# An attention and two feed-forward layers in one kernel: ScalarE's casts ordered behind its last copy, and one more block's rounding on VectorE

## The chip, the cores and the metric

The kernel runs on one core of a Trainium2 chip. The core has TensorE (PE in the profile; its weight loads are PEld), VectorE (DVE), ScalarE (ACT), GpSimd (POOL) and SyncE (SP), which issues all transfers of this kernel. Each engine works through its own queue strictly in order; an instruction that waits holds up all that stand behind it on its engine. The metric is the device time of one execution in microseconds (us), lower is better; the median of several runs is compared.

## The reference

Three parts follow each other, all in float32, on 4 x 576 = 2304 tokens of width 512.

```python
B, H, S, D = 4, 8, 576, 64
scores = (1.0 / np.sqrt(D)) * np.matmul(q, k.transpose(0, 1, 3, 2))
cum = np.cumsum(np.maximum(s, 0.0), axis=-1)
bias = -(cum[:, :, :, None] - cum[:, :, None, :])
scores = np.where(causal, -1e9, scores + np.minimum(bias, 0.0))
attn = softmax(scores)                       # max subtracted, sum + 1e-9
x = np.matmul(attn, v)                       # -> (2304, 512)
h = x @ w_in                                 # 512 -> 2048
x = (h - np.tanh(h)) @ w_out                 # 2048 -> 512
h = (x @ w1) * (x @ w2) @ w3                 # 512 -> 1024 -> 1024
out = h @ w_out2                             # 1024 -> 512
```

## The kernel before

**Stages.** The first phase (to about 385 us) does attention and, woven into it, the first half of the first feed-forward layer: 8 of the 16 slices of w_in and w_out. The second phase does the other 8 slices (tiles named hb, yb) and prepares weights; the third does the second feed-forward layer. The change touches the first phase alone.

**Attention.** Work goes by pairs of heads, numbered 0 to 31 (`p.n`); pairs 0 to 7 are of the first batch and are computed without a split (`p.first`). For a pair, TensorE makes score tiles `s` in PSUM; VectorE takes the maxima (`nm`); ScalarE takes the exponentials (`pr`) and their sums; TensorE transposes them (`pt`); ScalarE copies the transposes to SBUF (`pf`, line 310; from the second batch on VectorE copies those of unit B2); TensorE multiplies them with v (`pv`); VectorE multiplies `pv` by the inverted sums `rb`, which come back through DRAM (`rt`, `rd`, `rb`), and so writes x into `xy` (line 364). From pair 8 on GpSimd adds most of the bias (`pr`, line 206, two to four operations a pair) and sets the causal mask (line 218). All tiles `s`, `pt`, `pv` and `pri` share five PSUM banks.

**Feed-forward.** x is taken in nine blocks of 256 tokens (blk 0 to 8), each as four column chunks. For full precision every operand is split in two float32r parts, a rounded high part and the rest, and every product is three matmuls (high by high, high by low, low by high). `cut_x` splits a chunk of x into `xhl`: ScalarE casts the high part (line 64), VectorE subtracts for the low part (line 65). For each of 8 slices f of a block TensorE makes `h` (12 matmuls over the four chunks in order), ScalarE takes tanh (`th`, line 460), VectorE subtracts (line 463), g is split into `gh` and `gl`, and TensorE adds g times w_out to `y`. `split` casts on ScalarE and subtracts on GpSimd, unless told otherwise; blocks 0 and 1 split g that way, blocks 2 to 8 do both on VectorE:

```python
if blk < 2:
    split(gh, gl, t)
else:
    split(gh, gl, t, hi=nc.vector.tensor_copy, lo=nc.vector.tensor_sub)
```

**Weights.** `convert` turns raw 64-bit weights into float32 on VectorE in three operations (lines 88, 91 and 93, tile `cvt`), casts the high part on ScalarE and subtracts on GpSimd. `park` does the same for weights that are written to DRAM until the second phase (`park_win`, `park_wout`).

**Order.** TensorE's order is written out by hand (a table of steps, `at`). The other engines' order is set by a scheduler that goes by its own estimate of times; `in_turn(i, behind)` adds an order between two instructions that it must keep (no semaphore is waited for, it only restrains where the scheduler may place i). So casts and copies stand on ScalarE where the scheduler expects them to be ready.

Of the kernel before, what the change touches and what calls it, by code (L numbers as in the profile page):

```python
# [15 lines left out]
P = 128  # L16
# [8 lines left out]
BLK = 256  # L25
# [12 lines left out]
def tile_kernel(ctx: ExitStack, tc: tile.TileContext, qk, v, s, w_in, w_out, w1, w2, w3t, w_o2, outT):  # L38
    nc = tc.nc
# [10 lines left out]
    xy = cp.tile([P, NC, NT], F32, tag="xy", name="xy")  # L50
# [45 lines left out]

    def convert(raw, name, w=None, lo=None, behind=None):
        t = plain(raw, name, behind)
        w = slot(name) if w is None else w
        split(w[:, 0, :], w[:, 1, :], t, lo=lo)  # L100
        return w
# [21 lines left out]
    with ExitStack() as actx:  # L123
# [20 lines left out]

        latest, least, last_exp, paces = [None], [None], [None], []
        PACED = 70
# [159 lines left out]
        def evacuate(p, j, e):  # L306
            pieces, pt, at = p.pf[j, e]

            pf = a2.tile([P, {"B1": 512, "B2": 416}.get(j, 384)], F32, tag=f"pf{0 if j == 'A' else j[1]}".replace("3", "0"), name=f"pf{p.n}_{j}_{e}")
            (nc.vector.tensor_copy if j == "B2" and not p.first else nc.scalar.copy)(pf[:, :at], pt[:, :at])  # L310
            p.pf[j, e] = pieces, pf, at
# [28 lines left out]
        def store(p):  # L340
            m = 2 * p.ni
            p.rt = a2.tile([6, P], F32, tag="rt", name=f"rt{p.n}")
            nc.scalar.copy(p.rt[:m], p.pt[:m, :P])
            p.rd = dr.tile([2, 3 * P], F32, tag="rd", name=f"rd{p.n}", bufs=4)
            nc.sync.dma_start(p.rd[:, :p.ni * P].rearrange("t (i c) -> t i c", c=P), p.rt[:m])
# [23 lines left out]
        def conversions(fs):  # L369
# [5 lines left out]
            for m, (d, f, src, n) in enumerate(todo):  # L375
                d[f] = convert(raws.pop(0), n, behind=least[0])
                if m + 2 < len(todo):
                    raws.append(load_raw(*todo[m + 2][2:], behind=latest[0]))
                yield
# [20 lines left out]
        def ffn():  # L400
# [6 lines left out]
            def cut_x(blk, lo):  # L407
                xs = cut.setdefault(blk, [])
                c, c0 = len(xs), blk * BLK
                x = f2.tile([P, 2, BLK], F32R, tag="xhl", name=f"xhl{blk}_{c}", bufs=6)  # L410
                split(x[:, 0, :], x[:, 1, :], xy[:, c, c0:c0 + BLK], lo=lo)
                xs.append(x)

            for blk in range(NB):
# [30 lines left out]
                for f in range(F1):  # L445
# [16 lines left out]
                    def rest(t=t, hh=hh, gh=gh, gl=gl, blk=blk):  # L462
                        nc.vector.tensor_sub(t, hh, t)  # L463
                        if blk < 2:
                            split(gh, gl, t)
# [561 lines left out]
```

## Time and profile before

| | us |
|---|---|
| median of 3 runs | 954.67 |
| lowest and highest | 949.22, 955.17 |
| the profiled execution | 953.33 |
| its span, first to last instruction | 951.5 |

The profile is of one execution: 1.8 us of its own time lie outside its span. The rows further below are of that execution, and times in them count from the start of the span. PE was busy in 97% of the span at a mean granted clock of 0.989; DVE in 68%, ACT in 48%, POOL in 24%. A row of the timeline has its start, its duration, engine, line, operation, what it writes and reads with shapes, and in square brackets how long the engine sat idle before it and what released it. Buffer numbers are left out of names there.

### The profile page before, as it was taken

Reading aid. Unit: us, or ns where it says so; the run is one execution under the profiler, and the core shown is the slowest. Engines: PE = TensorE matmul, PEld = TensorE weight load, DVE = VectorE, ACT = ScalarE, POOL = GpSimd, SP = SyncE. Lnnn points to the kernel's source line nnn. Section 1 sums busy time; section 2 is a strip of 40 time slices with the busy share of each in tenths; the row PEclk is TensorE's granted clock in tenths of the full one; section 3 lists DMA queues with packets and bytes.
Section 4 is the critical chain, followed back from the end, with each engine's and each line's share of the span. In section 5 each row is a group of like instructions: output and inputs, shape, how many; then the busy total and the mean of one; then the engine's idle time right before and its main releaser. Section 6 shows DMA issues by size and latency. Waiting matters only on the chain.

```text
span 951.5 us, 16425 instructions
## 1 busy us (share of the span) xinstructions
PE 921.0 (97%) x6022; PEld 803.0 (84%) x6025; DVE 646.5 (68%) x1394; ACT 452.2 (48%) x1061; POOL 231.0 (24%) x219
## 2 busy tenths in 40 slices
PE   8889999899999999999999999998999999999998
PEld 4467778788888889998888888986899999999997
DVE  7677767687787866767999887673145546744654
ACT  4457877777777743324544343332124232433233
POOL 2245756556565410000000000020024111311100
PEclk9799999999999999999999999999999999999999
DMA  5555365435444523499788644668399767776746
GB/s 161 192 160 171 112 199 189 170 126 183 147 167 145 179 91 98 147 355 362 265 287 302 215 146 177 220 268 295 118 323 332 285 238 288 269 268 234 274 174 218
DMA packets 59648, 203.41 MB, mean 214 GB/s; under 512 B 6608, under 2 KB 21104, under 8 KB 53424
## 3 DMA queue, kind: packets, MB, share of 16 engines
q1 hardware_dynamic: 59568, 202.37, 61.2%
q8 instruction: 47, 0.77, 0.3%
q14 instruction: 33, 0.27, 0.1%
HBM read 153.95 MB, written 48.39 MB: 213 GB/s over the span
## 4 chain that ended last, share of the span: by engine, by line
PE 77%; DVE 9%; DMA 6%; issue 3%; ACT 3%; POOL 1%; SPq 1%; ACTq 0%; DVEq 0%; POOLq 0%
PE yb L117 10%; PE hb L117 10%; PE h L117 8%; PE W L849 8%; PE y L431 7%; PE oW L906 5%; PE w3o L117 4%; PE s_B L229 4%; PE Y L849 4%; PE pv L327 4%; PE oY L906 4%; PE pt_B L301 3%; DVE tso L885 2%; DMA cb<-cum_d 1%; PE V L849 1%
## 5 line engine op out<-in xcount | busy, mean ns | idle before, releaser
L117 PE MATMUL h<-xhl,win 128*128 128x256 f32 x864 | 121.2, 286 | 2.7 <-DVE xhl L65 2.2
L117 PEld LDWEIGHTS h<-xhl,win 128*128 128x128 f32 x864 | 106.2, 188 | 13.7 <-issue 3.9
L117 PE MATMUL hb<-x,win 128*128 128x512 f32 (+1 forms) x480 | 104.9, 367 | 0.0
L117 PEld LDWEIGHTS hb<-x,win 128*128 128x128 f32 x480 | 83.9, 188 | 15.0
L117 PE MATMUL yb<-ghb,wout 128*128 128x512 f32 (+1 forms) x320 | 95.6, 367 | 0.0
L206 POOL TENSOR_SCALAR pr<-cb,cq 128x384 f32<-128x384 f32 (+1 forms) x48 | 89.1, 1869 | 25.0 <-DMA cb<-cum_d 15.2
L431 PE MATMUL y<-gh,wout 128*128 128x256 f32 x576 | 85.5, 288 | 0.0
L290 ACT ACTIVATE pr<-pr,nm 128x128 f32<-128x128 f32 (+2 forms) x120 | 71.5, 598 | 18.6 <-DVE nm L268 18.4
L431 PEld LDWEIGHTS y<-gh,wout 128*128 128x128 f32 x576 | 72.8, 189 | 3.0 <-issue 2.0
L65 POOL TENSOR_TENSOR B11hl<-xy,B11hl 128x768 fp32r<-128x768 f32 x3 | 5.8, 1931 | 276.8 <-ACT B11hl L64 276.8
L117 PEld LDWEIGHTS yb<-ghb,wout 128*128 128x128 f32 x320 | 58.2, 188 | 9.9
L117 PE MATMUL yb<-glb,wout 128*128 128x512 f32 (+1 forms) x160 | 58.4, 367 | 0.0
L301 PE MATMUL pt_B<-ident,pr 96*128 96x96 f32 (+1 forms) x384 | 52.3, 260 | 1.9 <-DVE xy L364 1.0
L967 POOL TENSOR_TENSOR xy<-c,c 128x384 f32<-128x384 f32 x12 | 15.3, 1278 | 148.7 <-DVE c L958 148.7
L117 PE MATMUL w3o<-wo,w3b 128*128 128x512 f32 x192 | 46.0, 400 | 3.9 <-DMA w3b<-w_d 3.9
L268 DVE CUSTOM_DVE_ANT_0 pr<-s_B,pr 96x512 f32<-96x512 f32 (+1 forms) x72 | 44.2, 638 | 8.0 <-PE s_B L229 7.8
L431 PE MATMUL y<-gl,wout 128*128 128x256 f32 x288 | 45.4, 280 | 3.8 <-POOL gl L65 3.8
L117 PEld LDWEIGHTS w3o<-wo,w3b 128*128 128x128 f32 x192 | 36.9, 194 | 12.4 <-issue 4.6
L301 PEld LDWEIGHTS pt_B<-ident,pr 96*128 96x128 f32 (+1 forms) x384 | 41.9, 144 | 6.3 <-issue 3.4
L310 ACT COPY pf_B<-pt_B 128x512 f32<-128x512 f32 (+2 forms) x72 | 35.8, 499 | 22.7 <-PE pt_B L301 22.7
L463 DVE TENSOR_TENSOR th<-h,th 128x256 f32<-128x256 f32 x72 | 30.0, 417 | 22.5 <-ACT th L460 21.7
L460 ACT ACTIVATE th<-h 128x256 f32<-128x256 f32 x72 | 26.9, 374 | 35.3 <-PE h L117 35.3
(213 smaller groups left out, 2093.6 us busy)
## 6 DMA issues: line engine op xcount, KB each, us to landing
S<-wg_d SPq DMA_DIRECT2D x24, 1024.0 KB
wo<-wo_d SPq DMA_DIRECT2D x42, 512.0 KB
A<-wg_d SPq DMA_DIRECT2D x24, 768.0 KB
qk<-in_qk SPq DMA_DIRECT2D x16, 576.0 KB
raw_win<-in_w_in SPq DMA_DIRECT2D x16, 512.0 KB
raw_wout<-in_w_out SPq DMA_DIRECT2D x16, 512.0 KB
raw_w<-in_w SPq DMA_DIRECT2D x16, 512.0 KB
wg_d<-pks SPq DMA_DIRECT2D x8, 1024.0 KB
```

Source lines behind the costliest of these rows:

```text
L117: i = nc.tensor.matmul(ps, a, b, start=first and n == 0, stop=last and n == 2, skip_group_check=skip)
L206: nc.gpsimd.tensor_scalar(out=t[:pw, e, :w], in0=p.cb[:pw, e, :w], scalar1=c, scalar2=0.0, op0=ALU.add, op1=ALU.min)
L229: latest[0] = nc.tensor.matmul(ps[e][:PW[i], o:o + k1 - k0], w[r, 0, CH0[i]:CH0[i] + PW[i]], x[r, 1, k0:k1], start=z == 0 and (not p.first ...
L268: least[0] = nc.vector.tensor_tensor_reduce(out=t[:pw, k0:k1], in0=ps[:pw, o:o + k1 - k0], in1=t[:pw, k0:k1], scale=-0.125, scalar=nm[:pw, ...
L290: last_exp[0] = nc.scalar.activation(t[:pw, :], t[:pw, :], AF.Exp, bias=m, scale=-1.0, accum_out=p.sums[:pw, e, c:c + 1])
L301: nc.tensor.transpose(pt[:, at:at + pw], p.pr[i][:pw, e, KC0[kj]:KC0[kj] + P], ident[:pw, :pw])
L310: (nc.vector.tensor_copy if j == "B2" and not p.first else nc.scalar.copy)(pf[:, :at], pt[:, :at])
L327: nc.tensor.matmul(p.pv[D * e:D * e + D, c:p.nq], p.vs[:, e, kj], pf[:, beg:end], start=z == 0, stop=z == len(todo) - 1, skip_group_check= ...
L431: nc.tensor.matmul(o, wout[f][:, z, P * c:P * c + P], x, start=f == 0 and n == 0 and c % 2 == 0, stop=f == F1 - 1 and n == 2, skip_group_c ...
L463: nc.vector.tensor_sub(t, hh, t)
L849: i = nc.tensor.matmul(ps[:, :T], w[:, x, P * j:P * j + P], b[:, y, j], start=first and j == n == 0, stop=stop and j == 1 and n == 2, skip ...
L906: nc.tensor.matmul(ps[:, :T], w[:, a, q % 2, P * j:P * j + P], x[:, b, q], start=o in ("B11", "B21", "T1") and q == z == 0, stop=o in ("T4 ...
```

## The change

`copied[0]` remembers ScalarE's latest copy of transposes (`pf`, or `rt` of line 343). Two kinds of cast on ScalarE are then ordered behind the copy that was last recorded when they are recorded: those of the chunks of x (`cut_x`) and those of the converted weights that stay in SBUF (`conversions`; not the parked ones). VectorE's low halves follow the casts. And the split of g in block 1 goes from ScalarE and GpSimd to VectorE, as in blocks 2 to 8.

```diff
--- before.py
+++ after.py
@@ -94,10 +94,10 @@
                                        op0=ALU.bitwise_and, op1=ALU.bitwise_or)
         return t.bitcast(F32)
 
-    def convert(raw, name, w=None, lo=None, behind=None):
+    def convert(raw, name, w=None, lo=None, behind=None, after=None):
         t = plain(raw, name, behind)
         w = slot(name) if w is None else w
-        split(w[:, 0, :], w[:, 1, :], t, lo=lo)
+        in_turn(split(w[:, 0, :], w[:, 1, :], t, lo=lo), after)
         return w
 
     def park(raw, name, dst, pool, behind):
@@ -142,7 +142,7 @@
 
         REL = ((0, 0), (0, P), (1, 0), (1, 384), (0, 384))
 
-        latest, least, last_exp, paces = [None], [None], [None], []
+        latest, least, last_exp, copied, paces = [None], [None], [None], [None], []
         PACED = 70
 
         def paced(i):
@@ -307,7 +307,10 @@
             pieces, pt, at = p.pf[j, e]
 
             pf = a2.tile([P, {"B1": 512, "B2": 416}.get(j, 384)], F32, tag=f"pf{0 if j == 'A' else j[1]}".replace("3", "0"), name=f"pf{p.n}_{j}_{e}")
-            (nc.vector.tensor_copy if j == "B2" and not p.first else nc.scalar.copy)(pf[:, :at], pt[:, :at])
+            if j == "B2" and not p.first:
+                nc.vector.tensor_copy(pf[:, :at], pt[:, :at])
+            else:
+                copied[0] = nc.scalar.copy(pf[:, :at], pt[:, :at])
             p.pf[j, e] = pieces, pf, at
 
         def products(p, j):
@@ -340,7 +343,7 @@
         def store(p):
             m = 2 * p.ni
             p.rt = a2.tile([6, P], F32, tag="rt", name=f"rt{p.n}")
-            nc.scalar.copy(p.rt[:m], p.pt[:m, :P])
+            copied[0] = nc.scalar.copy(p.rt[:m], p.pt[:m, :P])
             p.rd = dr.tile([2, 3 * P], F32, tag="rd", name=f"rd{p.n}", bufs=4)
             nc.sync.dma_start(p.rd[:, :p.ni * P].rearrange("t (i c) -> t i c", c=P), p.rt[:m])
 
@@ -373,7 +376,7 @@
                 raws.append(load_raw(*todo[m][2:], behind=latest[0]))
                 yield
             for m, (d, f, src, n) in enumerate(todo):
-                d[f] = convert(raws.pop(0), n, behind=least[0])
+                d[f] = convert(raws.pop(0), n, behind=least[0], after=copied[0])
                 if m + 2 < len(todo):
                     raws.append(load_raw(*todo[m + 2][2:], behind=latest[0]))
                 yield
@@ -408,7 +411,7 @@
                 xs = cut.setdefault(blk, [])
                 c, c0 = len(xs), blk * BLK
                 x = f2.tile([P, 2, BLK], F32R, tag="xhl", name=f"xhl{blk}_{c}", bufs=6)
-                split(x[:, 0, :], x[:, 1, :], xy[:, c, c0:c0 + BLK], lo=lo)
+                in_turn(split(x[:, 0, :], x[:, 1, :], xy[:, c, c0:c0 + BLK], lo=lo), copied[0])
                 xs.append(x)
 
             for blk in range(NB):
@@ -461,7 +464,7 @@
 
                     def rest(t=t, hh=hh, gh=gh, gl=gl, blk=blk):
                         nc.vector.tensor_sub(t, hh, t)
-                        if blk < 2:
+                        if blk < 1:
                             split(gh, gl, t)
                         else:
                             split(gh, gl, t, hi=nc.vector.tensor_copy, lo=nc.vector.tensor_sub)
```

TensorE's order is the same in both kernels. On the other engines instructions are moved in the first 380 us alone. In the rows below a number in a tile's name is that of its pair or of its block and chunk (`xhl1_2` is chunk 2 of block 1); the long number at the end is the buffer's. Lines from 310 on are up to 3 higher in the changed kernel.

ScalarE near 28 to 35 us, before:

```order
L310 COPY pf2_A_0_426<-pt2_A_0_398 128x384
L64 CAST xhl0_0_591<-xy_71 128x256
L310 COPY pf2_A_1_450<-pt2_A_1_431 128x384
L64 CAST xhl0_1_594<-xy_71 128x256
L64 CAST win1_412<-cvt_win1_408 128x512
L64 CAST wout1_465<-cvt_wout1_461 128x512
L343 COPY rt3_475<-pri3_459 4x128
L310 COPY pf3_A_0_479<-pt3_A_0_455 128x384
L310 COPY pf3_A_1_513<-pt3_A_1_481 128x384
```

and now:

```order
L313 COPY pf2_A_0_426<-pt2_A_0_398 128x384
L313 COPY pf2_A_1_450<-pt2_A_1_431 128x384
L64 CAST win1_412<-cvt_win1_408 128x512
L64 CAST wout1_465<-cvt_wout1_461 128x512
L346 COPY rt3_475<-pri3_459 4x128
L313 COPY pf3_A_0_479<-pt3_A_0_455 128x384
L313 COPY pf3_A_1_513<-pt3_A_1_481 128x384
```

The casts of chunks 0 and 1 of block 0 are gone from here (they stand some 25 instructions later, before pair 5's first exponentials); both weight casts keep their place ahead of `rt3` and the copies of pair 3.

VectorE where block 1 begins (115 to 120 us; `ISA` with `nm10` are the maxima of pair 10, `cvt_win8` a parked weight), before:

```order
L268 ISA pr10_1_1419,nm10_1520<-s10_A_1_1490,pr10_1_1419 128x256
L268 ISA nm10_1520 128x1
L333 TENSOR_SCALAR rw1_97<-sums9_1308 128x6
L88 TENSOR_SCALAR cvt_win8_1599<-raw_win8_1359 128x512
L334 RECIPROCAL rw1_97<-rw1_97 128x6
L65 TENSOR_TENSOR xhl1_3_1544<-xy_71,xhl1_3_1544 128x256
L91 SCALAR_TENSOR_TENSOR cvt_win8_1599<-raw_win8_1359,cvt_win8_1599 128x512
L93 SCALAR_TENSOR_TENSOR cvt_win8_1599<-raw_win8_1359,cvt_win8_1599 128x512
L364 TENSOR_TENSOR xy_71<-pv8_1563,rb8_1400 128x256
L333 TENSOR_SCALAR rw0_96<-sums10_1533 128x4
```

and now:

```order
L337 RECIPROCAL rw1_97<-rw1_97 128x6
L268 ISA pr10_1_1419,nm10_1520<-s10_A_1_1490,pr10_1_1419 128x256
L268 ISA nm10_1520 128x1
L88 TENSOR_SCALAR cvt_win8_1599<-raw_win8_1359 128x512
L65 TENSOR_TENSOR xhl1_0_1514<-xy_71,xhl1_0_1514 128x256
L65 TENSOR_TENSOR xhl1_1_1538<-xy_71,xhl1_1_1538 128x256
L91 SCALAR_TENSOR_TENSOR cvt_win8_1599<-raw_win8_1359,cvt_win8_1599 128x512
L65 TENSOR_TENSOR xhl1_2_1541<-xy_71,xhl1_2_1541 128x256
L65 TENSOR_TENSOR xhl1_3_1544<-xy_71,xhl1_3_1544 128x256
L93 SCALAR_TENSOR_TENSOR cvt_win8_1599<-raw_win8_1359,cvt_win8_1599 128x512
```

All four low halves of block 1's chunks now stand here, two on either side of the middle step of the weight's conversion; chunks 0, 1 and 2 stood about 100, 65 and 15 instructions earlier.

VectorE where block 2 begins (176 to 182 us), before:

```order
L91 SCALAR_TENSOR_TENSOR cvt_win10_2498<-raw_win10_2269,cvt_win10_2498 128x512
L93 SCALAR_TENSOR_TENSOR cvt_win10_2498<-raw_win10_2269,cvt_win10_2498 128x512
L333 TENSOR_SCALAR rw0_96<-sums16_2455 128x4
L334 RECIPROCAL rw0_96<-rw0_96 128x4
L364 TENSOR_TENSOR xy_71<-pv14_2466,rb14_2325 128x256
L65 TENSOR_TENSOR xhl2_3_2514<-xy_71,xhl2_3_2514 128x256
L268 ISA pr17_3_2428,nm17_2537<-s17_B1_0_2480,pr17_3_2428 96x512
L268 ISA nm17_2537 96x1
L268 ISA pr17_3_2428,nm17_2537<-s17_B1_1_2481,pr17_3_2428 96x512
L268 ISA nm17_2537 96x1
```

and now:

```order
L93 SCALAR_TENSOR_TENSOR cvt_win10_2498<-raw_win10_2269,cvt_win10_2498 128x512
L367 TENSOR_TENSOR xy_71<-pv14_2466,rb14_2325 128x256
L336 TENSOR_SCALAR rw0_96<-sums16_2455 128x4
L65 TENSOR_TENSOR xhl2_0_2505<-xy_71,xhl2_0_2505 128x256
L65 TENSOR_TENSOR xhl2_1_2508<-xy_71,xhl2_1_2508 128x256
L337 RECIPROCAL rw0_96<-rw0_96 128x4
L65 TENSOR_TENSOR xhl2_2_2511<-xy_71,xhl2_2_2511 128x256
L268 ISA pr17_3_2428,nm17_2537<-s17_B1_0_2480,pr17_3_2428 96x512
L268 ISA nm17_2537 96x1
L268 ISA pr17_3_2428,nm17_2537<-s17_B1_1_2481,pr17_3_2428 96x512
L268 ISA nm17_2537 96x1
L65 TENSOR_TENSOR xhl2_3_2514<-xy_71,xhl2_3_2514 128x256
```

Here three low halves come behind the last step of the conversion and x of pair 14, and the fourth behind the two maxima of pair 17 instead of ahead of them. ScalarE's casts of these chunks stand together likewise: chunks 0 to 2 behind the last exponential of pair 16, chunk 3 behind `pf15_B1_1` and the cast of `park_win10`. Eight casts `gh1_0` to `gh1_7` leave ScalarE and eight subtractions `gl1_0` to `gl1_7` leave GpSimd; on VectorE each pair follows its `th1` closely.

## Rows read from the trace of the kernel before

**Rows 1.** Waits of PE, 28 to 182 us: total, times, longest.

```profile
PE y L431 <- POOL gl L65: 3.8, 2, 2.4
PE s_B L229 <- ACT rt L343: 2.9, 1, 2.9
PE h L117 <- DVE xhl L65: 1.9, 2, 1.4
```

**Rows 2.** Timeline of PE: start, duration, idle before in brackets.

```profile
34.48 2.28 PE L229 MATMUL s_B<-qk 64*128 64x384 f32 x8 [2.89 <-ACT rt L343]
...
117.03 0.50 PE L117 MATMUL h<-xhl,win 128*128 128x256 f32 x2 [0.52 <-DVE xhl L65]
...
137.38 0.74 PE L431 MATMUL y<-gl,wout 128*128 128x256 f32 x4 [1.36 <-POOL gl L65]
...
176.66 0.98 PE L431 MATMUL y<-gl,wout 128*128 128x256 f32 x4 [2.44 <-POOL gl L65]
...
181.08 1.68 PE L117 MATMUL h<-xhl,win 128*128 128x256 f32 x12
```

**Rows 3.** Stretches: busy us of each engine, granted PE clock, DMA share.

```profile
32.00:34.00 2.00, 0.00 (x0) 0.00 (x0) 2.00 (x5) 1.37 (x3) 0.59 (x1) 0.90 0.35 71
46.00:48.00 2.00, 2.00 (x7) 0.51 (x6) 1.86 (x4) 1.77 (x7) 0.00 (x0) 0.69 0.22 90
176.00:178.00 2.00, 1.34 (x6) 0.99 (x8) 1.58 (x4) 0.70 (x2) 2.00 (x3) 0.74 0.00 0
178.00:180.00 2.00, 2.00 (x13) 1.30 (x9) 0.42 (x1) 0.00 (x0) 1.85 (x4) 0.50 0.03 8
180.00:182.00 2.00, 2.00 (x15) 1.45 (x14) 0.87 (x2) 0.89 (x2) 0.00 (x0) 0.91 0.61 244
182.00:204.00 22.00, 22.00 (x195) 18.76 (x194) 17.88 (x54) 16.37 (x45) 10.34 (x11) 1.00 0.51 182
```

**Rows 4.** Timeline of DVE, 28 to 36 us.

```profile
32.60 0.42 DVE L65 TENSOR_TENSOR xhl<-xy,xhl 128x256 fp32r<-128x256 f32 x1
32.94 0.68 DVE L93 SCALAR_TENSOR_TENSOR cvt_wout<-raw_wout,cvt_wout 128x512 uint32<-128x512 uint32 x1
33.54 1.49 DVE L65 TENSOR_TENSOR xhl<-xy,xhl 128x256 fp32r<-128x256 f32 x1
```

**Rows 5.** Timelines of ACT and POOL, 28 to 36 us.

```profile
34.18 0.25 ACT L343 COPY rt<-pri 4x128 f32<-4x128 f32 x1
...
33.41 1.33 POOL L65 TENSOR_TENSOR win<-cvt_win,win 128x512 fp32r<-128x512 f32 x1 [8.24 <-ACT win L64]
```

**Rows 6.** Timeline of DVE where block 1 begins.

```profile
116.59 0.38 DVE L65 TENSOR_TENSOR xhl<-xy,xhl 128x256 fp32r<-128x256 f32 x1
116.89 1.59 DVE L91 SCALAR_TENSOR_TENSOR cvt_win<-raw_win,cvt_win 128x512 uint32<-128x512 uint32 x1
```

**Rows 7.** Timeline of POOL in block 1.

```profile
128.20 7.70 POOL L206 TENSOR_SCALAR pr<-cb,cq 128x384 f32<-128x384 f32 x4 [6.28 <-DMA cb<-cum_d]
...
175.45 1.15 POOL L65 TENSOR_TENSOR gl<-th,gh 128x256 fp32r<-128x256 f32 x1
```

**Rows 8.** Timeline of DVE where block 2 begins.

```profile
176.05 1.10 DVE L93 SCALAR_TENSOR_TENSOR cvt_win<-raw_win,cvt_win 128x512 uint32<-128x512 uint32 x1
...
181.47 0.68 DVE L268 CUSTOM_DVE_ANT_0 pr<-s_B,pr 96x512 f32<-96x512 f32 x1
```

**Rows 9.** Groups by line and shape, DVE, 182 to 350 us: busy, mean ns, idle before.

```profile
L65 DVE TENSOR_TENSOR gl<-th,gh 128x256 fp32r<-128x256 f32 x30 | 16.2, 541 | 0.7
...
L64 DVE CAST gh<-th 128x256 fp32r<-128x256 f32 x30 | 12.2, 405 | 0.8
...
L65 DVE TENSOR_TENSOR xhl<-xy,xhl 128x256 fp32r<-128x256 f32 x14 | 8.2, 589 | 3.0 <-ACT xhl L64 3.0
```

**Rows 10.** Timelines of PE and DVE where block 6 begins.

```profile
354.54 2.17 PE L117 MATMUL h<-xhl,win 128*128 128x256 f32 x12
...
355.71 0.43 DVE L65 TENSOR_TENSOR xhl<-xy,xhl 128x256 fp32r<-128x256 f32 x1 [0.66 <-ACT xhl L64]
```

## The prediction

> **What bounds the kernel now.** I read the stretches first. From 182 us on to the end of the first phase TensorE is busy without a gap at full clock [rows 3], and behind it the order of all engines is untouched. TensorE's own order and work are the same in both kernels. So the change can only win or lose what TensorE waits for before 182 us, what its clock loses through those waits, and a few block starts later. The second view is the list of TensorE's waits from 28 to 182 us [rows 1]; I then looked up each wait in the timeline, where the bracket names what ended it [rows 2]. Four of them lie where the change works: 2.89 us for ScalarE's `rt` before 34.48, 0.52 us for VectorE's low half of x where block 1 begins, and 1.36 and 2.44 us for GpSimd's low half of g in block 1. Two of the waits are followed or accompanied by a fall of the granted clock to half. In the slice from 32 to 34 us the mean is 0.90, which puts the first fall at 33.6; in the slice from 46 to 48 it is 0.69, which puts its end at 47.25. The second fall spans 176 to 182 us, with means of 0.74, 0.50 and 0.91 [rows 3]. It takes 2 x (0.26 + 0.50 + 0.09) = 1.7 us of full-clock time, from a TensorE that had work throughout.
>
> **Part 1, the casts near 30 us.** ScalarE no longer stops at chunk 1 of block 0, but the next two in its queue are the casts of `win1` and `wout1`, still ahead of `rt3`, for which TensorE waits. They need VectorE's last conversion steps, and those stand behind x of pair 1, as before. All that is saved is one low half between the two conversion steps on VectorE: 32.94 - 32.60 = 0.34 us [rows 4]. So `rt3`, at 34.18 [rows 5], comes at about 33.84, and TensorE goes on at 34.14. The clock had fallen at 33.6, when TensorE is idle in both kernels, so the fall stays. Term: -0.34, between -0.7 and 0.
>
> **Part 2, where block 0 begins (48 to 52 us).** Chunks 0 to 2 come later on both engines, but `h0_0` waits for chunk 3, whose low half stands behind the same conversion step and the same maxima as before. Term: 0, give or take 0.4. Later in block 0 a copy (`pf4_B3_1`) goes behind six exponentials, but by the order the bank that TensorE then takes is freed by one of these exponentials instead, so nothing is charged.
>
> **Part 3, where block 1 begins.** Before, the last low half ended at 116.59 + 0.38 = 116.97 [rows 6] and TensorE went on at 117.03. Now VectorE does two low halves, a conversion step, and two more, behind the same `cvt_win8` step, which ended just before 116.59. An undisturbed low half takes 0.34 from start to start and a conversion step 33.54 - 32.94 = 0.60 [rows 4], so the fourth ends later by three low halves and the step, 3 x 0.34 + 0.60 = 1.6 us, if nothing holds VectorE up. The step itself took 1.59 us here [rows 6], which makes it 2.6. From this goes up to 0.4, since VectorE gets here a little earlier without chunk 2's low half: +1.2 to +2.6, and I take +1.6, as the row of the step overlaps GpSimd operations that will not all be there at the same moment. In these 3 us or so TensorE gets its chunks one by one. Whether its clock falls then I can't read: it fell after the wait of 2.44 us and did not after that of 1.36 [rows 2, 3]. I price a fall at the 1.7 us above with a chance of one half: +0.85.
>
> **Part 4, low part of g in block 1.** GpSimd's subtraction waited in its queue behind four bias operations that took 7.70 us [rows 7], and the second one, at 175.45, behind two more. With both steps on VectorE right behind `th1`, TensorE finds `gl` ready: -1.36 and -2.44, and the clock's fall after the second goes as well, -1.70. Sum -5.5. The price is 8 casts of 405 ns and 8 subtractions of 541 ns on VectorE [rows 9], 7.6 us spread over some 60 us. I cost this at nothing: block 2 does exactly this already, and there VectorE is busy for 17.88 of 22.00 us while TensorE has no gap [rows 3]. If the cover were gone, it would cost as in the second rival. ScalarE and GpSimd only lose work, and GpSimd's masks come earlier by the subtractions that stood ahead of them (up to 1.15 us each, [rows 7]).
>
> Here the Trainium skill speaks against the change. The row shows a low half of 1.49 us instead of 0.42 that starts while GpSimd works from 33.41 to 34.74 [rows 4, 5]. The page "SBUF — State Buffer", section "Who interferes with whom", says that a VectorE instruction with two SBUF inputs contends with a GpSimd instruction that reads SBUF, one fully blocking the other. The trace agrees. By that rule alone each of the 8 subtractions could be held once more, as in the second rival; the mean of 541 ns against 0.42 undisturbed says that in blocks 2 to 5 this happens to few of them.
>
> **Part 5, where block 2 begins.** Without the wait and the slow clock TensorE would reach `h2_0` at 181.08 - 2.44 - 1.70 = 176.94 and be through at 178.6. But VectorE's queue is now longer here. Its last conversion step ended at 176.05 + 1.10 = 177.15 [rows 8]; a cast and a subtraction more ahead of it (0.95) and a low half less (0.59 by the mean, [rows 9]) make that about 177.5. Then come x of pair 14 (0.34), `rw0` and a reciprocal (0.4 together, an estimate by their few columns against a low half), three low halves (1.0), two maxima (2 x 0.65, [rows 8]) and the fourth low half (0.4): 3.4 us, to 180.9, and `h2_0` ends 0.3 later at 181.2. That is +2.6 against 178.6; with every step at its shortest +1.5, with a step held by GpSimd +3. I take +2.4. Again TensorE idles in pieces that add up to over 2 us, so again half of 1.7: +0.85. The net of parts 4 and 5 is what a reader should watch: a wait for GpSimd becomes a wait for VectorE.
>
> **Part 6, later blocks.** Blocks 3, 5, 7 and 8 have their chunks long before they begin. In block 6 `h6_0` already took 2.17 us instead of 1.68 [rows 2, 10] because its last low half starts at 355.71; two more low halves ahead of x of pair 30, less one earlier, add about 0.3, and block 4 has a low half behind a maximum with little slack: +0.4, between 0 and 1.
>
> **The sum.** -0.34 + 1.6 + 0.85 - 5.5 + 2.4 + 0.85 + 0.4 = +0.3 us on the profiled execution of 953.33: 953.6. That execution is 1.3 us below the median of 954.67, well inside the spread of the three runs (949.22 to 955.17); I predict 953.5. A measurement of this kernel tells about 1%, 9.5 us, from no change.
>
> **Rivals.**
> 1. The gain is kept. The scheduler put the low halves where it thinks there is time; if VectorE gets there early enough, no block start waits: -0.34 - 5.5 = -5.8, that is 947.5. For it speaks that blocks 3 and 5 begin without a wait; against it that the four low halves of block 1 and 2 stand behind work that in the trace ended only when TensorE was already there.
> 2. Slower: VectorE blocked by GpSimd in block 1. The place is the subtraction `gl1`, between `th1` and the maxima; in that stretch GpSimd has long bias operations (1.9 us each, [rows 7]). Each subtraction held once costs 1.49 - 0.42 = 1.07 us, and the maxima behind it free TensorE's banks late. It decides once VectorE's delay exceeds its idle share, 4.1 of 22 us in block 2. If six of the eight reach TensorE: 953.6 + 6.4 = 960.0. Against it: block 2.
> 3. The clock at 33.6 does not fall or comes back early, as TensorE resumes sooner. It would give back half of 47.25 - 33.6 = 13.65 us: 953.6 - 6.8 = 946.8. Against it: the fall comes before either kernel's wait ends.
> 4. The change doesn't do what it says. In part it does not: the wait for `rt3` stays, since the weight casts stay ahead of it. This is in the forecast.
>
> **How the numbers follow.** The forecast, from 950 to 957.5 by the bounds of its terms (both clocks kept: 951.9; both lost and all upper ends: 957.5), has 0.62; rival 1 0.15, rival 2 0.13, rival 3 0.04, and 0.06 is left for what I don't see. The range from 947 to 960 holds the forecast, most of rival 1 and rival 2. Faster by over 1% (below 945.1) needs rivals 1 and 3 together: 0.08. Slower by over 1% (above 964.2) needs rival 2 at all eight and both clocks: 0.07. Within: 0.85.
>
> **What the profile after would show.** No wait of TensorE for POOL `gl` in block 1; waits for DVE `xhl` of over 1 us in sum where blocks 1 and 2 begin, the second behind two maxima; the wait for ACT `rt` near 34 us at about 2.55 us with the clock falling at the same time; from block 3 on TensorE without gaps. I am wrong if the waits at the block starts are missing, if the maxima of block 1 come late behind `gl1`, or if the clock near 34 us stays up.

## The result and the profile after

The changed kernel takes 956.87 us in the median of 15 runs (951.86 to 962.55), the kernel before 951.05 in 15 runs beside it (946.91 to 955.17). The ratio is 1.0064, 95% interval 1.0045 to 1.0083: it is slower by 6.1 us, a little over half a per cent. (The three runs shown ahead of the prediction had a median of 954.67; more runs put that lower.) I had forecast no change, +0.3 us. Of the 6.1 us some 0.4 lie outside the span: the changed kernel's runs have 2.2 us there, those of the kernel before 1.8.

The profiled execution after takes 956.08 us with a span of 953.9, 2.4 us more than the one before. I set each matmul of the one beside the same matmul of the other. First the three longest rows of the list of TensorE's waits from 28 to 182 us, then rows of its timeline (start, duration, idle before in brackets), both of the changed kernel:

```profile
PE h L117 <- DVE xhl L65: 3.6, 3, 1.5
PE s_B L229 <- DVE nm L268: 2.4, 1, 2.4
PE s_B L229 <- ACT rt L346: 1.7, 1, 1.7
```

```profile
34.07 1.42 PE L229 MATMUL s_B<-qk 64*128 64x384 f32 x8 [1.68 <-ACT rt L346]
50.12 0.51 PE L117 MATMUL h<-xhl,win 128*128 128x256 f32 x2 [1.55 <-DVE xhl L65]
...
115.39 1.17 PE L117 MATMUL h<-xhl,win 128*128 128x256 f32 x6 [1.22 <-DVE xhl L65]
117.41 1.44 PE L117 MATMUL h<-xhl,win 128*128 128x256 f32 x5 [0.85 <-DVE xhl L65]
...
142.02 0.74 PE L229 MATMUL s_B<-qkh 64*96 64x512 f32 x1 [2.40 <-DVE nm L268]
...
182.25 1.36 PE L117 MATMUL h<-xhl,win 128*128 128x256 f32 x9 [0.70 <-DVE xhl L65]
184.54 0.50 PE L117 MATMUL h<-xhl,win 128*128 128x256 f32 x2 [0.94 <-DVE xhl L65]
```

Against [rows 1, 2] the waits for GpSimd's `gl` are gone and those for VectorE's `xhl` have grown, as forecast. The wait of 2.40 us for the maxima `nm` is new. The prediction names it among the signs of being wrong, and it is not in the forecast. The granted clock, by stretches of the same kernel (busy us of TensorE, granted clock, DMA share, GB/s):

```profile
34.00:36.00 2.00, 1.93 (x11) 0.84 0.93 330
...
44.00:46.00 2.00, 2.00 (x8) 0.60 0.48 189
...
116.00:118.00 2.00, 1.15 (x6) 0.82 0.00 0
118.00:120.00 2.00, 2.00 (x12) 0.50 0.00 0
120.00:122.00 2.00, 2.00 (x16) 0.83 0.00 0
...
140.00:142.00 2.00, 0.00 (x0) 0.79 0.22 90
142.00:144.00 2.00, 1.98 (x7) 0.50 0.43 172
144.00:146.00 2.00, 2.00 (x12) 0.50 0.63 168
146.00:148.00 2.00, 2.00 (x11) 0.50 0.98 405
```

The fall near 177 us [rows 3] is gone. The one near 34 us is still there, but in this execution it begins at 35.4, after TensorE has gone on at 34.07. New are two: the clock falls behind the start of block 1 (3.4 us at half) and behind the wait for `nm` (141.2 to 148, 6.8 us at half). The step from matmul to matmul against before: 1.4 us ahead at 107 us, 2.0 behind after the start of block 1, 0.5 ahead at 137, 2.8 behind after the wait for `nm`, 5.3 behind at 148, level at 180.5, 2.2 behind once block 2 has begun, and 2.4 at the end.

That explains one pair of executions. It does not explain the medians, which lie 5.8 us apart. For that each run's own span and mean granted clock are needed. Of the kernel before there are 123 such runs beside the experiments, and 12 more in before_again; of the changed one there are 22.

### The profile page after: what moved, and what is told of

Same layout as the page of the kernel before. It is cut to its first block, busy times and chain, and to the rows that moved or that the text cites. A ratio compares the mean times of both kernels' runs of the same rounds, so it can differ in the third digit from the quotient of the medians.

```text
span 953.9 us, 16414 instructions
## 1 busy us (share of the span) xinstructions
PE 925.6 (97%) x6022; PEld 805.1 (84%) x6025; DVE 647.3 (68%) x1410; ACT 449.6 (47%) x1053; POOL 224.5 (24%) x211
## 4 chain that ended last, share of the span: by engine, by line
PE 78%; DVE 9%; DMA 6%; ACT 3%; issue 3%; POOL 0%; SPq 0%; ACTq 0%; DVEq 0%; POOLq 0%
PE yb L117 10%; PE hb L117 10%; PE h L117 10%; PE y L434 9%; PE W L852 7%; PE oW L909 5%; PE w3o L117 4%; PE s_B L229 4%; PE pv L330 4%; PE oY L909 4%; PE Y L852 4%; PE pt_B L301 3%; DVE tso L888 2%; DMA cb<-cum_d 1%; DVE nm L257 1%
## 5 line engine op out<-in xcount | busy, mean ns | idle before, releaser
L117 PE MATMUL h<-xhl,win 128*128 128x256 f32 x864 | 124.5, 290 | 5.9 <-DVE xhl L65 5.3
L117 PEld LDWEIGHTS h<-xhl,win 128*128 128x128 f32 x864 | 108.4, 191 | 17.9 <-DVE xhl L65 6.7
L206 POOL TENSOR_SCALAR pr<-cb,cq 128x384 f32<-128x384 f32 (+1 forms) x48 | 91.1, 1912 | 30.1 <-DMA cb<-cum_d 18.8
```

Of the source, the lines that this page charges most:

```text
L117: i = nc.tensor.matmul(ps, a, b, start=first and n == 0, stop=last and n == 2, skip_group_check=skip)
L206: nc.gpsimd.tensor_scalar(out=t[:pw, e, :w], in0=p.cb[:pw, e, :w], scalar1=c, scalar2=0.0, op0=ALU.add, op1=ALU.min)
```

## The experiments

All timed kernels, 7 to 15 runs each. "Its clock" is the mean of the granted clock over its runs; "lost" is the mean of span times one minus clock, what the clock would cost if every stretch at half clock were lost in full. The experiments were run in four groups, each on another chip and each beside runs of the kernel before; "clock beside" is that of these runs.

| kernel | ratio to before | interval | its clock | clock beside | lost, us | span x clock, us |
|---|---|---|---|---|---|---|
| before, 123 runs in all | 1 | | 0.9901 | | 9.4 | 940.2 |
| after, first 15 runs | 1.0064 | 1.0045 to 1.0083 | 0.9859 | not recorded | 13.5 | 941.4 |
| after_again | 1.0074 | 1.0040 to 1.0108 | 0.9859 | 0.9912 | 13.5 | 940.9 |
| before_again | 1.0001 | 0.9978 to 1.0025 | 0.9916 | 0.9912 | 8.0 | 941.4 |
| g_alone | 0.9985 | 0.9963 to 1.0007 | 0.9922 | 0.9912 | 7.4 | 939.5 |
| order_alone | 1.0067 | 1.0038 to 1.0095 | 0.9860 | 0.9912 | 13.4 | 942.0 |
| order_block0 | 1.0024 | 1.0002 to 1.0047 | 0.9868 | 0.9895 | 12.5 | 939.7 |
| order_block1 | 1.0030 | 1.0007 to 1.0052 | 0.9882 | 0.9895 | 11.2 | 940.2 |
| order_block2 | 1.0000 | 0.9980 to 1.0021 | 0.9907 | 0.9895 | 8.8 | 941.0 |
| order_late | 0.9999 | 0.9975 to 1.0022 | 0.9907 | 0.9895 | 8.8 | 940.3 |
| after_filled | 1.0031 | 1.0013 to 1.0050 | 0.9922 | 0.9910 | 7.4 | 943.3 |
| after_fill_0 | 1.0025 | 1.0002 to 1.0047 | 0.9895 | 0.9889 | 10.0 | 941.6 |
| after_fill_1 | 1.0039 | 1.0019 to 1.0059 | 0.9886 | 0.9889 | 10.9 | 941.7 |
| after_from2 | 0.9962 | 0.9935 to 0.9989 | 0.9927 | 0.9889 | 7.0 | 939.6 |
| before_filled | 0.9975 | 0.9956 to 0.9994 | 0.9953 | 0.9910 | 4.5 | 941.7 |
| g_alone_filled | 0.9968 | 0.9950 to 0.9986 | 0.9967 | 0.9910 | 3.2 | 941.6 |

Two readings of these runs bound what the clock explains. Over the 123 runs of the kernel before, the span goes up by 6.8 us where the mean clock goes down by 0.01, not by the 9.5 us that "lost" counts; so "lost" overstates the price by some 40%. And at the same clock the changed kernel is still slower: 25 runs of the kernel before at 0.987 have spans of 951.5 us on the mean, 7 of the changed one 953.7. So of the 6.1 us some 3 are the clock (0.0042 at 6.8 us per 0.01), 2 to 3 are there at equal clock, and 0.4 lie outside the span.

### The two kernels again

Both kernels unchanged, for second profiles and each run's clock.

**before_again.** 

> The kernel before once more, for a second profile and for how its time varies. Theory (the clock makes the difference between executions): times lie on one line against the mean granted clock, some 9.5 us for 0.01, and the second profile has fewer or other stretches of half clock than the first, so that the profiled 953.33 is not typical of the median of 951.05. Rival (work and waits vary): the clock is the same in all and TensorE's waits differ by 2 us or more. Ratio 0.998 to 1.002 either way.

**after_again.** 

> The changed kernel once more. Theory (held cast): the cast of gh1_1 on VectorE again takes about 2 us instead of 0.3 while GpSimd works through its masks and a weight's low part, TensorE waits about 2.4 us for the maxima behind it, and the clock falls there; ratio 1.005 to 1.008. Rival (accident of one execution): the cast takes 0.3 us, no wait for nm, and the loss of the medians comes from the block starts alone.

Before: ratio 1.0001. Its runs went from 946.03 us at a clock of 1.000 to 954.89 at 0.986, so time goes with the clock, as the theory had it, but not on one line: span times clock is 938.1 to 945.3. The other half of that expectation is mixed: the second profile's fall near 34 us was shorter, but it had one more, near 137 us, behind a wait for `gl` of 2.05 us; both profiled executions were slower than their median. After: 1.0074, the held cast is there again (2.75 us), and the wait for `nm` behind it was 2.69 us. This time no fall followed that wait, while the falls behind 34 us and block 1's start were there again. So the same kernel meets the same wait and the clock falls in one execution and not in the other.

### The two parts apart

```diff
@@ g_alone: before.py
-                        if blk < 2:
+                        if blk < 1:
@@ order_alone: after.py
-                        if blk < 1:
+                        if blk < 2:
```

**g_alone.** 

> The kernel before with only the second part of the change: block 1's g split on VectorE, casts ordered as before. My prediction's terms: both waits for gl and the clock's fall after the second go, nothing comes in their place: -5.5 us, ratio 0.994. Theory now (held cast takes the gain back): -1.4 -2.4 -1.7 and +2.4 for the maxima behind a held cast, with a fall of the clock of up to 3.4 behind it: -3 to 0 us, ratio 0.997 to 1.000. Rival (the split is what costs): slower, ratio 1.003 or more.

**order_alone.** 

> The kernel before with only the first part: casts of x and of converted weights ordered behind the last copy, block 1's g as before on ScalarE and GpSimd. Theory (the ordering costs at the block starts): chunks late at blocks 1 and 2, some +1.7 +1.7 (clock) at block 1, +2.2 at block 2, -1.2 near 34 us: +4.4 us, ratio 1.003 to 1.007. Rival (block starts only take the place of gl waits): ratio 0.999 to 1.001, with the waits for gl shorter by what the block starts wait more.

The ordering alone costs what the whole change costs (1.0067). In its profile TensorE waits 1.22 and 0.84 us for chunks where block 1 begins and 0.67 where block 2 begins, and not at all for `gl`. That much is what the rival expected, but the rival's ratio of 1 is excluded. (That execution, at 951.19 us, is the fastest of its twelve.) The split of g alone brings 0.9985, which is -1.4 us (-3.5 to +0.7), not -5.5. The theory of the held cast gave -3 to 0. In the profile of g_alone the row is

```profile
140.67 0.47 PE L229 MATMUL s_B<-qkh 64*96 64x512 f32 x1 [1.25 <-DVE nm L268]
```

Such a wait for `nm`, of 1.25 to 2.69 us, between 135 and 144 us, stands in all eight profiles of kernels with block 1's g on VectorE, and in none of the eight without.

### The ordering block by block

Only the casts of some blocks are ordered, the weights' casts are not, and block 1's g stays as before. No run has the ordering of the weights' casts alone.

```diff
@@ after.py, with blk < 2 for g (order_block0; the others have blk == 1, blk == 2, blk > 2)
-                d[f] = convert(raws.pop(0), n, behind=least[0], after=copied[0])
+                d[f] = convert(raws.pop(0), n, behind=least[0])
...
-                in_turn(split(x[:, 0, :], x[:, 1, :], xy[:, c, c0:c0 + BLK], lo=lo), copied[0])
+                in_turn(split(x[:, 0, :], x[:, 1, :], xy[:, c, c0:c0 + BLK], lo=lo), copied[0] if blk == 0 else None)
```

**order_block0.** 

> Of the ordering only the casts of block 0's chunks; all other casts and block 1's g as before. Theory (block starts 1 and 2 carry the loss, through a clock that falls at their waits in most executions): little here, -1.2 us from the wait near 34 us, ratio 0.997 to 1.001. Rival (the start of block 0 carries it, by a fall of the clock between 50 and 56 us): ratio 1.003 or more, mean granted clock under 0.989.

**order_block1.** 

> Only the casts of block 1's chunks ordered. Theory: the largest part, +1.7 of waits at the block's start and 1.7 to 3.4 of clock, +3.4 us, ratio 1.0035 (1.002 to 1.005), mean granted clock 0.987 to 0.989 against 0.991 before. Rival (block starts only replace waits for gl): ratio 0.999 to 1.001.

**order_block2.** 

> Only the casts of block 2's chunks ordered. Theory: waits of 2.2 us at the block's start, of which the wait for gl just before hides nothing, and as much of clock as before: +2 us, ratio 1.002 (1.000 to 1.004). Rival (VectorE has room there): ratio 0.999 to 1.001.

**order_late.** 

> Only the casts of the chunks of blocks 3 to 8 ordered. Theory (TensorE has no gap there in either kernel): no change, ratio 0.999 to 1.001, clock 0.991. Rival (a late block start costs in executions that the profiles do not show): ratio 1.002 or more.

Block 1 costs 1.0030 as expected (the plain means of its 12 runs and the 35 beside them lie 1.4 us apart, so it may be less). Block 2 costs nothing, where I had expected +2 us, and neither do the later ones. Block 0, which I had put at nothing, costs 1.0024: its rival is the nearer one. The four add to 0.0053, order_alone has 0.0067; whether the rest is the weights' ordering, the four together, or noise is open. Against the runs beside them order_block0 loses 2.6 us more to the clock (0.7 to 4.4), order_block1 1.2 (-1.3 to 3.6), so for block 1 the clock is not shown by its own runs. The profile of order_block0 shows how block 0 can lose; it is of an execution of 957.31 us, the second slowest of the twelve (median 953.23). Timeline of TensorE, then the stretches:

```profile
49.59 0.79 PE L117 MATMUL h<-xhl,win 128*128 128x256 f32 x2 [2.33 <-DVE xhl L65]
```

```profile
46.00:48.00 2.00, 1.25 (x11) 1.00 0.45 46
48.00:50.00 2.00, 0.41 (x2) 0.80 0.56 225
50.00:52.00 2.00, 2.00 (x10) 0.50 0.41 63
...
60.00:62.00 2.00, 2.00 (x9) 0.50 0.77 202
62.00:64.00 2.00, 2.00 (x16) 0.78 0.43 175
```

Behind a wait of 2.33 us TensorE has work, but runs at half clock for 13.7 us: of the eight stretches of 2 us the first lacks 0.20 of its clock, six lack 0.50 and the last 0.22, which is 6.8 us of full-clock time. But the wait is no mark of the ordering. In order_block2, whose casts of block 0 are not ordered, it is

```profile
50.59 0.50 PE L117 MATMUL h<-xhl,win 128*128 128x256 f32 x2 [2.56 <-DVE xhl L65]
```

and 3.4 us at half clock follow. In both profiles the fall near 34 us was the shorter one, 6.8 us instead of the 10.2 or 13.7 of the other profiles without added matmuls, so TensorE came to this wait 13.4 and 13.3 us behind the end of its wait near 34 us, in the changed kernel 14.5.

### Unread matmuls in the waits

If the clock is the main cost, work put into the waits can make the kernel faster. The matmuls write where nobody reads: the unused half of `h`'s bank, or a spare bank.

```diff
@@ after_filled: after.py (after_fill_0 and after_fill_1 have the first, or the other two, of these)
                     for c in range(NC):
+                        for _ in range({(0, 0, 3): 12, (1, 0, 0): 10, (1, 0, 2): 7}.get((blk, f, c), 0)):
+                            nc.tensor.matmul(ph[:, BLK:2 * BLK], win[0][:, 0, :P], win[0][:, 0, :BLK], start=False, stop=False, skip_group_check=True)
@@ before_filled: before.py, with {(0, 0, 3): 11} there, and in scores (g_alone_filled: both in g_alone)
+            if p.n == 4 and j == "B3":
+                for _ in range(7):
+                    nc.tensor.matmul(spare, win[0][:, 0, :P], win[0][:, 0, :], start=True, stop=True)
```

**after_filled.** 

> The changed kernel, with 29 matmuls whose result nobody reads, put where TensorE waits at the starts of blocks 0 and 1: 12 ahead of chunk 3 of block 0, 10 ahead of chunk 0 and 7 ahead of chunk 2 of block 1 (256 columns each, some 0.11 us). They lie within the waits of 1.55, 1.22 and 0.85 us. Theory (the ordering loses through the clock that falls at these two starts in most executions): work is added and the time goes down, back to about the kernel before: ratio 0.998 to 1.002, mean granted clock 0.989 to 0.992 instead of 0.986. Rival (the waits themselves, or falls elsewhere): ratio 1.005 to 1.010, clock 0.986.

**before_filled.** 

> The kernel before, with 7 such matmuls of 512 columns (0.37 us each) ahead of the scores that wait for rt3 near 34 us, and 11 of 256 columns ahead of chunk 3 of block 0. Theory (a wait costs twice, the second time through the clock): the stretch of half clock behind 34 us, 10 to 14 us long, goes in most executions: -5 to -7 us, ratio 0.993 to 0.995, clock 0.996 to 0.998. Rival (the clock falls for another reason than TensorE's idle time): ratio 0.999 to 1.002, clock 0.991.

**g_alone_filled.** 

> The kernel with only block 1's split of g moved, and the same 18 matmuls as in the kernel before. Theory: both gains add, ratio 0.991 to 0.994. Rival (VectorE's split brings its own falls of the clock, by the held cast near 139 us): no better than the kernel before with the same matmuls.

after_filled: with 29 matmuls more the kernel is some 3.5 us faster than the changed one (953.1 against after_again's 956.5, on another chip; by the ratios 3 to 4), and the clock is 0.9922, as expected and no lower than the 0.9910 beside it. The ratio of 1.0031 missed the 0.998 to 1.002: "lost" falls by 6 us, but span times clock grows by some 2 (3 against the runs beside it), since the waits did not shrink by all that was put in. At block 0 0.94 us were left, where the changed kernel has 1.55, behind 1.4 us of added matmuls. Where block 1 begins one wait is left of two:

```profile
117.67 0.50 PE L117 MATMUL h<-xhl,win 128*128 128x256 f32 x2 [0.62 <-DVE xhl L65]
```

before_filled: 0.9975, clock 0.9953. The direction is that of the theory, the size less than half: -2.4 us where -5 to -7 was expected. Stretches of its profile where the clock was at half before [rows 3]:

```profile
34.00:36.00 2.00, 2.00 (x18) 1.00 1.02 418
...
42.00:44.00 2.00, 2.00 (x10) 1.00 0.80 303
44.00:46.00 2.00, 2.00 (x20) 1.00 0.06 25
```

The long stretch is gone there; "lost" falls by 4.0 us against the runs beside it, and span times clock grows by 1.5. g_alone_filled (0.9968, clock 0.9967) missed its 0.991 to 0.994 likewise. It beats both kernels, but it lies only 0.0017 below g_alone and 0.0007 below before_filled, inside what the intervals leave open, so that both gains add is not shown.

### One start at a time, and without both

**after_fill_0.** 

> The changed kernel with the unread matmuls at the start of block 0 alone (12 of 256 columns ahead of chunk 3). Theory (both starts lose through the clock, in about equal parts): mean granted clock about 0.989 (0.986 without any, 0.992 with all 29), time lost to the clock about 10.5 us of 13.5; ratio 1.003 to 1.006. Rival (block 0 alone): clock 0.992, ratio 1.002 or less.

**after_fill_1.** 

> The changed kernel with the unread matmuls at the start of block 1 alone (10 ahead of chunk 0, 7 ahead of chunk 2). Theory (both starts in about equal parts): mean granted clock about 0.989, ratio 1.003 to 1.006. Rival (block 0 alone carries the loss): clock 0.986 and, as work is added, ratio 1.007 or more.

**after_from2.** 

> The changed kernel, but the casts of the chunks of blocks 0 and 1 are not ordered; from block 2 on they are, and block 1's g stays on VectorE. Theory (the two first block starts carry the loss): as block 1's g alone, ratio 0.9985 (0.996 to 1.001), mean granted clock 0.991 to 0.993. Rival (the ordering of later blocks costs once g is on VectorE too, as block 2's chunks then stand behind a longer queue): ratio 1.002 to 1.005, clock 0.989 or less.

```diff
@@ after_from2: after.py
-                in_turn(split(x[:, 0, :], x[:, 1, :], xy[:, c, c0:c0 + BLK], lo=lo), copied[0])
+                in_turn(split(x[:, 0, :], x[:, 1, :], xy[:, c, c0:c0 + BLK], lo=lo), copied[0] if blk > 1 else None)
```

Either half of the filling brings the clock to about 0.989, the number that "both in about equal parts" had named. But the kernel before has 0.9889 on this chip, and 0.9912 on that of after_again: either half alone already brings the clock back to that of the kernel before, give or take 2 us of "lost". What is left of the loss (1.0025 and 1.0039) lies in span times clock, 1.6 and 1.7 us against the runs beside, and outside the span, 0.5. So the shares of the two starts stay open. That block 0 carries the loss alone is excluded, since filling block 1 alone helps: 1.0039, up to 1.0059, where that rival had 1.007 or more. Each profile shows the start that was left open. after_fill_0, block 1, then after_fill_1, block 0:

```profile
117.49 1.44 PE L117 MATMUL h<-xhl,win 128*128 128x256 f32 x5 [0.86 <-DVE xhl L65]
```

```profile
116.00:118.00 2.00, 1.14 (x6) 0.68 0.00 0
118.00:120.00 2.00, 2.00 (x13) 0.50 0.00 0
...
126.00:128.00 2.00, 2.00 (x14) 0.76 0.97 241
```

```profile
50.41 0.50 PE L117 MATMUL h<-xhl,win 128*128 128x256 f32 x2 [1.91 <-DVE xhl L65]
```

```profile
52.00:54.00 2.00, 2.00 (x15) 0.50 0.81 237
...
60.00:62.00 2.00, 2.00 (x11) 0.50 0.81 256
62.00:64.00 2.00, 2.00 (x19) 0.95 0.10 39
```

Both are 10.2 us at half clock. after_from2, which has everything but the ordering at these two starts, is faster than the kernel before: 0.9962, clock 0.9927 (0.9889 beside it), no worse than g_alone. Its profile had no wait but the old one where block 1 begins:

```profile
117.59 0.50 PE L117 MATMUL h<-xhl,win 128*128 128x256 f32 x2 [0.45 <-DVE xhl L65]
```

So the loss goes with the ordering of the casts of blocks 0 and 1: without it none is left.

Counted over the 16 profiles: behind block 0's start the clock fell in 3 of 5 with its casts ordered and the wait not filled (3.4, 10.2 and 13.7 us at half; half of that lost, 2.7 us on the mean of five), in 3 of 7 without ordering (3.4 us each, 0.7 us on the mean), in none of 4 with the wait filled. In these 12 unfilled profiles it followed each of the six waits of 1.72 to 2.56 us and none of the six of 0.73 to 1.57; the waits are 1.84 us on the mean of the five with ordering and 1.54 of the seven without. Behind block 1's start it fell in 3 of 5 with ordering (3.4, 3.4, 10.2; 1.7 us on the mean) and in none of the 11 others. The difference of the means is 2.0 + 1.7 = 3.7 us, from few profiles; the runs have 4.1 us more "lost" (13.5 against 9.4 over all 123; 5.2 more than the 8.3 of the 30 taken beside after_again).

### What holds the cast

**probe_held.** 

> A kernel of its own that computes nothing of the reference: 16 stages, in each eight instructions of one kind on VectorE (a cast of 128x256 to float32r; a subtraction with both inputs in SBUF; a product with one input in PSUM; a maximum out of PSUM) beside four of one kind on GpSimd (nothing; the mask; the bias addition of 128x384; a subtraction of 128x512). Theory (held cast): casts that start beside masks or subtractions take as long as these are at it, 0.4 to 1.3 us instead of 0.3, and so do VectorE's subtractions; products and maxima with an input in PSUM keep their times. Beside the bias addition I expect VectorE's casts to be held as well, up to 1.9 us. Rival (the cast of 2.39 us was late for another reason): casts take 0.3 us beside everything.

First the place in the changed kernel, timelines of VectorE and GpSimd:

```profile
138.03 0.42 DVE L466 TENSOR_TENSOR th<-h,th 128x256 f32<-128x256 f32 x1 [1.14 <-ACT th L463]
138.48 2.39 DVE L64 CAST gh<-th 128x256 fp32r<-128x256 f32 x1
140.91 0.51 DVE L65 TENSOR_TENSOR gl<-th,gh 128x256 fp32r<-128x256 f32 x1
141.33 0.28 DVE L268 CUSTOM_DVE_ANT_0 pr<-s_A,pr 128x128 f32<-128x128 f32 x1
```

```profile
138.07 1.42 POOL L218 TENSOR_SCALAR_AFFINE_SELECT pr<-pr 128x256 f32<-128x256 f32 x4
139.46 1.26 POOL L65 TENSOR_TENSOR park_wout<-cvt_wout,park_wout 128x512 fp32r<-128x512 f32 x1
```

The cast `gh1_1` starts after the masks have begun and ends 0.15 us after the weight's low part does, at 140.87 against 140.72. Four maxima and TensorE's bank stand behind it. In the other profiles it is at times the subtraction `gl1_1` that is held instead (2.77 us in after_fill_1, the cast 0.29), or each of the two for a part (1.38 and 1.36 in after_from2). Then the probe, groups by line and shape (busy us, mean ns):

```profile
L65 DVE CAST cast_idle<-src 128x256 fp32r<-128x256 f32 x8 | 2.3, 292 | 0.2
L65 DVE CAST cast_mask<-src 128x256 fp32r<-128x256 f32 x8 | 3.0, 372 | 0.2
L65 DVE CAST cast_bias<-src 128x256 fp32r<-128x256 f32 x8 | 4.0, 500 | 0.2
L65 DVE CAST cast_diff<-src 128x256 fp32r<-128x256 f32 x8 | 6.4, 794 | 0.2
L68 DVE TENSOR_TENSOR sub_idle<-src,hi 128x256 fp32r<-128x256 f32 x8 | 3.4, 423 | 0.2
L68 DVE TENSOR_TENSOR sub_diff<-src,hi 128x256 fp32r<-128x256 f32 x8 | 7.2, 900 | 0.2
L71 DVE TENSOR_TENSOR mul_diff<-bank,src 128x256 f32<-128x256 f32 x8 | 3.4, 423 | 0.2
L73 DVE TENSOR_REDUCE max_diff<-bank 128x1 f32<-128x512 f32 x8 | 5.5, 690 | 0.2
```

Beside GpSimd's subtractions eight casts take 6.4 us instead of 2.3, so 4.0 of the 5.05 us of GpSimd's four subtractions are added to VectorE; beside four bias operations 1.7 us, beside four masks 0.6. Products and maxima with an input in PSUM keep their time beside everything (423 and 690 ns, as beside nothing). The cast is held like the subtraction, as the theory had it. It loses 0.50 us on the mean beside subtractions, the subtraction 0.48.

## Why the prediction was wrong

The time lies inside the range of 947 to 960, but no change was forecast and a loss came. **The step that failed** is the price of the ordering where blocks 0 and 1 begin. Parts 1, 2, 3 and 6 put the ordering there and near 34 us at -0.34 + 0 + 2.45 + 0.4 = +2.5 us; order_alone measured +6.4 (3.6 to 9.0). The term put at nothing without a reason is the clock in Part 2. The second failed step, the cover that Part 4 gave to VectorE's added work, hardly shows in the total, as told under Part 4.

**Part 1** (-0.34, the fall near 34 us stays): TensorE went on at 34.07 instead of 34.48, -0.41. The size is right. The fall stayed, but not for the reason given: it was not there while TensorE idled, it began at 35.4, 1.3 us after TensorE had gone on, and lasted 10.2 us instead of 13.7. The wait was 1.68 us, not 2.55.

**Part 2** (0, give or take 0.4): wrong. I looked for later chunks and found none, and gave the clock no price there. TensorE's wait was 1.55 us instead of 1.37, which is indeed nothing, but the ordering at this start costs 1.0024, 2.3 us (0.2 to 4.5), and it goes with the clock: 0.9868 against 0.9895 beside it, with span times clock at 939.7 and 940.0. Why the falls behind this start were longer with the ordering (up to 13.7 us) than without (3.4 each) is open; nothing I ran tells that apart.

**Part 3** (+1.6 and 0.85 for the clock): right as far as the runs tell. 1.22 + 0.85 us of waits against 0.52 are 1.55, and order_block1 gives 2.9 us (0.7 to 4.9) against 2.45. The half chance of a short fall was 3 of 5, one of them long (10.2 us, which would cost 5.1 and not 1.7).

**Part 4** (-5.5): wrong. The waits for `gl` went as forecast, and the fall at 177 us in the first pair of profiles. "I cost this at nothing: block 2 does exactly this already" does not hold in block 1, where VectorE's two steps of `g1_1` run into GpSimd's masks and a parked weight's low part and lose 1.3 to 2.6 us to them in the eight profiles. TensorE's wait for `nm` behind them is 1.8 us on the mean, and it can be followed by a fall of its own: from 130 to 190 us the eight profiles lose 1.5 us to half clock on the mean, the eight with g on ScalarE and GpSimd 2.1, so the clock gives back some 0.6 us instead of 1.70. g_alone puts the whole at -1.4 us (-3.5 to +0.7); after_from2, which also holds it, at -3.6 (-6.2 to -1.0). Those figures contain a wait for chunks where block 2 begins, so they stand against parts 4 and 5 together, -5.5 + 3.25 = -2.25. That this sum came near is luck: Part 4 was too good by some 3 us, and Part 5 too dear.

That was rival 2, with its mechanism right and its place and price wrong. I had six subtractions held for 1.07 us each, one GpSimd operation at a time; it is one place, where in the changed kernel VectorE got on only behind five operations in a row. And I had left the cast out: one input, so I did not look. The Trainium skill's page "SBUF — State Buffer", section "Who interferes with whom", names casts too among the instructions that can contend with GpSimd, in their fast modes. The probe agrees that casts are held: 292 ns undisturbed, 794 beside subtractions. Which mode the cast ran in no run shows.

**Part 5** (+2.4 and 0.85): the waits of 0.70 and 0.94 came and TensorE lost 2.2 us there in the profile. Alone the ordering at block 2 costs nothing (1.0000): the profile of order_block2 has the wait of 2.47 us for `gl` just ahead and none for a chunk. The wait for a chunk comes where that for `gl` is missing: 1.01 us in g_alone, without any ordering, and 0.67 in order_alone, without part 4.

**Part 6** (+0.4): order_late 0.9999. Nothing.

**The sum.** Without the clock the terms were -0.34 + 1.6 - 3.8 + 2.4 + 0.4 = +0.3, and span times clock moved from 940.2 to 941.4 and 940.9; at equal clock the runs are 2.2 us apart, so the waits balanced less well than forecast, and which of them that is stays open. Of the clock I had 0 in sum: a fall of 1.7 us less near 177, two half chances of 1.7 more. The runs say some 3 us by the slope of the kernel before, 4 to 5 by "lost". The mistake of method is that I read falls as if they belonged to the kernel. They differ from execution to execution: a single profile shows which waits may be followed by one, not how often. Two figures of the forecast don't come out either: the bounds of its terms add to 949.4 and 958.2, not 950 and 957.5, and rivals 1 and 3 together can't have 0.08 where rival 3 alone has 0.04.

## What to carry to other kernels

In a kernel like this one, with TensorE busy 97% of the time, a wait of it can cost twice, once as idle time and once through the clock. Price each new wait of a microsecond with a chance of a fall from several executions, and look at the mean clock of all runs before looking for microseconds in a single profile. Compare it with runs of the kernel before on the same chip: unchanged, it had 0.9889 on one and 0.9912 on another. A cast or subtraction moved to VectorE need not be hidden by VectorE's idle share if GpSimd has a row of SBUF operations queued at that moment: look at what GpSimd does in that very microsecond, not at the block that already works. Unread matmuls in waits that were left alone made the kernel before 0.25% faster, and 0.3% together with the split of g.

## What I had not expected of the hardware

The same kernel at the same wait lost its clock in one execution and kept it in the next (the wait for `nm`, 2.40 us with a fall and 2.69 us without; block 1's start with waits of 1.22 or 1.23 and some 0.85 us in four kernels, fallen in after and after_fill_0, not in order_alone and order_block1). The twelve runs of before_again ranged from 946.03 us at a mean clock of 1.000 to 954.89 at 0.986. That is 8.9 us, where the clock alone would make it 13: part of what a slow stretch takes is made up elsewhere, and no run shows where.

A VectorE cast that takes 0.29 us undisturbed took 2.39 us in the changed kernel and 2.82 in after_fill_0. In the changed kernel five GpSimd operations ran one behind the other meanwhile, and it ended only 0.15 us behind the last of them. In the probe, beside back-to-back GpSimd subtractions of 1.26 us, a cast took 0.79 us on the mean, so there some got in between.
